# Banks left in one copy on ScalarE, scaled rows in tiles of their own, and routing, census and gathers at other queue places

## The chip, the cores and the metric

The kernel runs on one core of a Trainium2 chip. The metric is the device time of one execution in microseconds (us); the median of three timed runs of the kernel before is 663.76 us (663.69 to 666.47). One more execution was profiled. TensorE is called PE in the rows, VectorE DVE, ScalarE ACT, GpSimd POOL, SyncE SP.

## The reference

Three layers follow each other: a linear attention with a norm, a mixture of eight experts with one expert for each token, and a max-out layer.

```python
kv = np.einsum('bhsd,bhse->bhde', k, v)          # 4 batches, 8 heads, 576 tokens, 64 wide
out = np.einsum('bhsd,bhde->bhse', q, kv)
x = out / sqrt(mean(out * out, -1) + 1e-06) * g_norm   # 2304 tokens x 512
expert_idx = np.argmax(x @ w_gate, axis=1)       # 512 x 8; gate weight from the softmax
# each expert takes its tokens in order, up to its capacity, and computes
y = relu(x @ w1[e]) @ w2[e]                      # 512 x 1024, 1024 x 512
out = gate_w * y[expert_idx, pos]
h = maximum(maximum(out @ m1, out @ m2), out @ m3)   # 512 x 768 each
result = h @ w_out                               # 768 x 512
```

## The kernel before

Each engine works through a queue in the order in which the kernel writes its instructions; waits between engines are semaphores that the framework derives from the tiles. The order is written out by hand.

**Attention, batches 0 to 3.** `kv_step(b)` forms k-transposed times v. `out_step(b)` transposes q and builds `kvx`, the block-diagonal product matrix with eight more columns per head, in which the gate weights are folded, so that one product gives 64 values and 8 gate logits per head (`LW` = 72). A batch has 576 tokens in five slices `s`: slice 0 has 64 rows, slices 1 to 4 have 128. `out_pair(b, u)` makes slices 1 and 2, or 3 and 4, in three groups of heads (three PSUM banks `po`): ScalarE squares the values (`sq`) and copies them to the row tile (`orow`), VectorE copies the logits to `olg` and sums the squares (`ss`). `out_rest(b)` does the same for slice 0.

**Norm and routing.** `stats_steps(b)` is a chain on VectorE (with one square root on ScalarE) that makes the row scales `rnorm`, scales the logits (`lt`, `lg`) and finds each token's expert as a one-hot row (`oh`). `normalise` scales the rows in place: for batches 0 to 2 five GpSimd instructions, for batch 3 split over ScalarE, GpSimd and VectorE. `route(b)` counts with TensorE (`pp`) and a few VectorE instructions where each token goes (`jr`, `pos_i`) and updates the running counts `ohsum`; `census(b)` takes from a product `pc` which expert comes first and how many of its tokens (`pb`) there are. `send(b)` puts five scatters (indirect DMAs that GpSimd issues, rows to `xs` in DRAM) in a list, and `drip` issues one of them behind an instruction of ScalarE, to spread them out.

**The first expert.** Its tokens don't wait for all scatters: for batches 0 and 1 `own_gather` fetches them from `xs` (indirect DMAs to `oxg`, which wait for all scatters so far) and `own_pe` transposes them; for batches 2 and 3 `own_pe` multiplies the scaled rows by 0/1 matrices (`picks`, made by `own`). The four results `px` go to `x0` by `own_out`. `keep_warm` runs idle products on TensorE. Then expert 0 starts (`ph`, the first product of the first layer), and the others follow; their weights come as `raw` tiles by SyncE's queue (four buffers) and are split in two by ScalarE and VectorE.

## Time and profile before

| | before |
|---|---|
| median of three runs | 663.76 us |
| the profiled execution | 663.60 us |
| its span, first to last instruction | 661.8 us |
| TensorE busy | 627.3 us (95%) |
| VectorE, ScalarE, GpSimd busy | 348.2, 270.0, 200.2 us |
| mean granted clock of TensorE | 0.97 |

The span is what the trace shows; 1.8 us of the execution lie around it. A granted clock of 1.00 is 2.4 GHz and one of 0.50 is 1.2 GHz. Busy shares are means over stages that have different limits, so they say where an engine has no room, not what a change is worth.

### The profile page before, as it was taken

Reading aid. Unit: us, or ns where it says so; the run is one execution under the profiler, and the core shown is the slowest. Engines: PE = TensorE matmul, PEld = TensorE weight load, DVE = VectorE, ACT = ScalarE, POOL = GpSimd, SP = SyncE. Lnnn points to the kernel's source line nnn. Section 1 sums busy time; section 2 is a strip of 40 time slices with the busy share of each in tenths; the row PEclk is TensorE's granted clock in tenths of the full one; section 3 lists DMA queues with packets and bytes.
Section 4 is the critical chain, followed back from the end, with each engine's and each line's share of the span. In section 5 each row is a group of like instructions: output and inputs, shape, how many; then the busy total and the mean of one; then the engine's idle time right before and its main releaser. Section 6 shows DMA issues by size and latency. Waiting matters only on the chain.

```text
span 661.8 us, 11400 instructions
## 1 busy us (share of the span) xinstructions
PE 627.3 (95%) x4141; PEld 600.5 (91%) x4141; DVE 348.2 (53%) x755; ACT 270.0 (41%) x619; POOL 200.2 (30%) x280
## 2 busy tenths in 40 slices
PE   7889699999999999999999999999999999999993
PEld 7778599998999999988999989989999999999992
DVE  1587726689898989889975421221231231231220
ACT  1674615685667575766754221121121121121110
POOL 3247553104576867768610001001001001001001
PEclk9999667999999999999999999999999999999997
DMA  8999334796697977887873000000000000000000
GB/s 221 290 280 279 123 116 150 220 298 208 215 273 260 272 239 253 283 248 267 230 202 96 1 17 32 1 17 33 0 17 33 0 17 33 0 17 33 1 16 34
DMA packets 81662, 88.11 MB, mean 133 GB/s; under 512 B 15357, under 2 KB 71165, under 8 KB 81602
## 3 DMA queue, kind: packets, MB, share of 16 engines
q1 hardware_dynamic: 68448, 66.64, 34.5%
q0 software_dynamic: 6240, 14.41, 6.1%
q10 hardware_dynamic: 6914, 6.30, 2.8%
q8 instruction: 34, 0.56, 0.4%
q14 instruction: 26, 0.21, 0.1%
HBM read 71.56 MB, written 15.76 MB: 132 GB/s over the span
## 4 chain that ended last, share of the span: by engine, by line
PE 81%; DVE 7%; DMA 4%; issue 2%; SPq 2%; ACT 2%; ACTq 0%; POOL 0%; POOLq 0%; DVEq 0%
PE pa L767 11%; PE pa L769 11%; PE pa L768 11%; PE ph L769 5%; PE ph L768 5%; PE ph L767 5%; PE py L768 5%; PE py L769 4%; PE py L767 4%; PE pz L1107 4%; PE pz L1106 4%; PE pz L1108 4%; PE px L662 3%; DVE w L298 2%; PE pxt L777 2%
## 5 line engine op out<-in xcount | busy, mean ns | idle before, releaser
L768 PE MATMUL pa<-ys,w 128*128 128x384 f32 x432 | 144.3, 334 | 0.0
L767 PE MATMUL pa<-ys,w 128*128 128x384 f32 x432 | 144.3, 334 | 0.0
L769 PE MATMUL pa<-ys,w 128*128 128x384 f32 x432 | 144.3, 334 | 0.0
L298 DVE TENSOR_TENSOR w<-raw,w 128x512 fp32r<-128x512 f32 x152 | 115.6, 789 | 23.1 <-ACT w L297 22.8
L1111 POOL DMA_INDIRECT out_dram<-o,ctab x18 | 17.5, 972 | 300.1 <-ACT o L1110 297.0
L1094 DVE TENSOR_TENSOR m<-pa,m 128x384 f32<-128x384 f32 x36 | 20.1, 558 | 138.3 <-PE pa L769 138.3
L297 ACT ACTIVATE w<-raw 128x512 fp32r<-128x512 f32 x152 | 89.4, 623 | 5.4 <-DMA raw<-in_moe_w_dram 5.4
L768 PE MATMUL py<-h,w 128*128 128x324 f32 (+7 forms) x256 | 79.9, 312 | 4.0 <-DVE h L791 4.0
L767 PE MATMUL ph<-xt,w 128*128 128x324 f32 (+7 forms) x256 | 80.7, 315 | 1.2 <-DVE xt L669 1.2
L768 PEld LDWEIGHTS pa<-ys,w 128*128 128x128 f32 x432 | 81.1, 188 | 0.2
L767 PEld LDWEIGHTS pa<-ys,w 128*128 128x128 f32 x432 | 81.1, 188 | 0.2
L769 PEld LDWEIGHTS pa<-ys,w 128*128 128x128 f32 x432 | 81.1, 188 | 0.0
L768 PE MATMUL ph<-xt,w 128*128 128x324 f32 (+7 forms) x256 | 80.4, 314 | 0.7 <-DVE xt L680 0.7
L1096 ACT ACTIVATE g<-m 128x384 fp32r<-128x384 f32 x36 | 18.9, 526 | 151.3 <-DVE m L1095 151.3
L769 PE MATMUL ph<-xt,w 128*128 128x324 f32 (+7 forms) x256 | 80.4, 314 | 0.0
L767 PE MATMUL py<-h,w 128*128 128x324 f32 (+7 forms) x256 | 79.9, 312 | 0.0
L769 PE MATMUL py<-h,w 128*128 128x324 f32 (+7 forms) x256 | 79.4, 310 | 0.0
L768 PEld LDWEIGHTS py<-h,w 128*128 128x128 f32 x256 | 48.3, 189 | 5.9 <-DVE h L791 5.9
L920 POOL TENSOR_TENSOR d<-d 128x256 f32<-128x256 f32 x48 | 32.8, 683 | 63.6 <-DVE d L919 15.5
L767 PEld LDWEIGHTS ph<-xt,w 128*128 128x128 f32 x256 | 49.3, 192 | 1.6 <-DVE xt L669 1.5
L768 PEld LDWEIGHTS ph<-xt,w 128*128 128x128 f32 x256 | 49.4, 193 | 1.1 <-DVE xt L680 1.0
L769 PEld LDWEIGHTS ph<-xt,w 128*128 128x128 f32 x256 | 49.3, 193 | 0.0
(252 smaller groups left out, 1055.1 us busy)
## 6 DMA issues: line engine op xcount, KB each, us to landing
raw<-in_moe_w_dram SPq DMA_DIRECT2D x64, 512.0 KB, 3.9
d<-in_moe_w_dram SPq DMA_DIRECT2D x36, 256.0 KB, 5.5
m2w<-dw ACTq DMA_DIRECT2D x36, 128.0 KB, 6.7
raw<-m2w SPq DMA_DIRECT2D x9, 512.0 KB, 4.7
k<-in_k_dram SPq DMA_DIRECT2D x8, 512.0 KB, 7.3
v<-in_v_dram SPq DMA_DIRECT2D x8, 512.0 KB, 9.4
q<-in_q_dram SPq DMA_DIRECT2D x8, 512.0 KB
d<-in_moe_w_out_dram SPq DMA_DIRECT2D x12, 256.0 KB, 5.5
```

Of the source, the lines that this page charges most:

```text
L297: nc.scalar.activation(out=hi, in_=src, func=AF.Copy)
L298: (eng or nc.vector).tensor_tensor(out=lo, in0=src, in1=hi.bitcast(F32), op=ALU.subtract)
L662: nc.tensor.matmul(px[:, dc], osb[b % 3][:n, s, 2 * dc:2 * dc + 2].rearrange("p h d -> p (h d)"), picks[b][:n, s], start=j == 0 and dc == ...
L767: nc.tensor.matmul(po, lhi, rhi, start=first, stop=False)
L768: nc.tensor.matmul(po, lhi, rlo, start=False, stop=False)
L769: nc.tensor.matmul(po, llo, rhi, start=False, stop=last)
L920: nc.gpsimd.tensor_tensor(out=lo.bitcast(F32), in0=hi.bitcast(F32), in1=lo.bitcast(F32), op=ALU.mult)
L1094: nc.vector.tensor_tensor(out=m_, in0=pa[1][:, :YB], in1=m_, op=ALU.max)
L1096: nc.scalar.activation(out=t_[:, 0], in_=m_, func=AF.Copy)
L1106: nc.tensor.matmul(po, h_[:, 0], w_[:, 0], start=c == 0, stop=False)
L1107: nc.tensor.matmul(po, h_[:, 0], w_[:, 1], start=False, stop=False)
L1108: nc.tensor.matmul(po, h_[:, 1], w_[:, 0], start=False, stop=c == NC2 - 1)
```

## The change

ScalarE's copy of a bank now takes all 72 columns to a new tile `ohl`, and VectorE's copies of the logits are gone; `stats_steps` reads the logits from `ohl`. `normalise` reads `ohl` and writes `orow`, which has two buffers in place of three. Routing, sending and the census product of the batch before are in pair 0 of a batch (hooks), no longer in pair 1 and behind it. Both gathers of the first expert's rows are made in batch 2, with one set of index instructions, ahead of that batch's statistics. In batch 3 the census and `own(2)` are a hook of pair 0, `own_pe` goes in the order 2, 0, 1, and `own_out` of these comes after the routing of batch 3. Three runs of `keep_warm` in batch 3 that were 10, 8 and 8 long are 8, 6 and 4 long. `po_f` and `po_i` are made after the stage.

```diff
@@ -312,13 +312,13 @@
         return wt[NT1 + 18 + c]
 
 
-    orow = [sl_.tile([128, 5, DM], F32, name=f"orow{b_}") for b_ in range(3)]
-    osb = [x.rearrange("p s (h d) -> p s h d", d=D) for x in orow]
+    ohl = [sl_.tile([128, 5, H, LW], F32, name=f"ohl{i}") for i in range(2)]
+    orow = [sl_.tile([128, 5, DM], F32, name=f"orow{i}") for i in range(2)]
     rnorm = [sl_.tile([128, 5, H], F32, name=f"rnorm{b_}") for b_ in range(B)]
-    olg = [sl_.tile([128, 5, H, NE], F32, name=f"olg{i}") for i in range(2)]
     ss = [sl_.tile([128, 5, H], F32, name=f"ss{i}") for i in range(2)]
     for i in range(2):
-        nc.gpsimd.memset(olg[i][D:128, 0], 0.0)
+        nc.gpsimd.memset(ohl[i][D:128, 0], 0.0)
+    for i in range(2):
         nc.vector.memset(ss[i][D:128, 0, :], 1.0)
     ohsum = sl_.tile([128, B + 1, NE], BF16, name="ohsum")
     nc.vector.memset(ohsum[:, 0, :], 0.0)
@@ -342,7 +342,7 @@
             if b == 0 and h % 4 == 0 and s == 1:
                 keep_warm(ps_o.tile([128, 512], F32, tag="po", name=f"warm{h}"), 4 if h else 9)
             if b == B - 1 and h == 4 and s == 1:
-                keep_warm(ps_o.tile([128, 512], F32, tag="po", name="warm3"), 10)
+                keep_warm(ps_o.tile([128, 512], F32, tag="po", name="warm3"), 8)
             l, r_ = (t_[h // 4][:, h % 4, s - 1, :] if s else t_[2][:, h, :] for t_ in (vt, kt))
             o_ = pk[h % 2 * D:h % 2 * D + D, h // 2, :]
             nc.tensor.matmul(o_, l, r_, start=s == 1 and h < 2, stop=s == 0 and h > 5)
@@ -388,7 +388,7 @@
             qT[u] = t_
 
         if b in (0, B - 1):
-            keep_warm(ps_o.tile([128, 512], F32, tag="po", name=f"warmq{b}"), 10 if b == 0 else 8)
+            keep_warm(ps_o.tile([128, 512], F32, tag="po", name=f"warmq{b}"), 10 if b == 0 else 6)
         tr(0)
         tr(2)
         if b == 0:
@@ -409,11 +409,9 @@
         nc.scalar.activation(out=sq, in_=po[:, :, 0:D], func=AF.Square)
         for i in range(2):
             d_ = slice(i * D, i * D + D)
-            i_ = nc.scalar.activation(out=osb[b % 3][0:D, 0, i::2], in_=po[d_, :, 0:D], func=AF.Copy)
+            i_ = nc.scalar.activation(out=ohl[b % 2][0:D, 0, i::2], in_=po[d_], func=AF.Copy)
             nc.vector.tensor_reduce(out=ss[b % 2][0:D, 0, i::2], in_=sq[d_], axis=AX.X, op=ALU.add)
         drip(b, i_)
-        for i in range(2):
-            nc.vector.tensor_copy(olg[b % 2][0:D, 0, i::2], po[i * D:i * D + D, :, D:LW])
 
     class Pair:
 
@@ -443,11 +441,8 @@
             nc.scalar.activation(out=self.sq[:, h0:h1], in_=self.po[g][:, :, :, 0:D], func=AF.Square)
 
         def copy(self, g):
-            return nc.scalar.activation(out=self.at(osb, g).rearrange("p r h c -> p h r c"),
-                                        in_=self.po[g][:, :, :, 0:D], func=AF.Copy)
-
-        def logits(self, g):
-            nc.vector.tensor_copy(self.at(olg, g).rearrange("p r h c -> p h r c"), self.po[g][:, :, :, D:LW])
+            return nc.scalar.activation(out=self.at(ohl, g).rearrange("p r h c -> p h r c"),
+                                        in_=self.po[g], func=AF.Copy)
 
         def reduce(self, g):
             h0, h1 = self.groups[g]
@@ -462,7 +457,6 @@
                 hooks[g]()
             pr.square(g)
             drip(b, pr.copy(g))
-            pr.logits(g)
         nc.vector.tensor_reduce(out=ss[b % 2][:, 1 + 2 * u:3 + 2 * u, :].rearrange("p r h -> p h r"),
                                 in_=pr.sq, axis=AX.X, op=ALU.add)
 
@@ -488,7 +482,7 @@
         V.scalar_tensor_tensor(out=r_, in0=u, scalar=1.5, in1=r0, op0=ALU.add, op1=ALU.mult)
         yield
         lt = tmp("lt", [H, NE])
-        V.tensor_tensor(out=lt, in0=olg[b % 2][:, t0:t1], in1=r_.unsqueeze(3).to_broadcast([128, n, H, NE]),
+        V.tensor_tensor(out=lt, in0=ohl[b % 2][:, t0:t1, :, D:LW], in1=r_.unsqueeze(3).to_broadcast([128, n, H, NE]),
                         op=ALU.mult)
         yield
         l_, m_ = lg[:, b, t0:t1], mx[:, b, t0:t1]
@@ -510,13 +504,16 @@
     def rows_of(s):
         return 128 if s else D
 
-    def normalise(o_, r_, n, eng):
-
+    def normalise(b, s, eng):
+
+        n = rows_of(s)
+        i_ = ohl[b % 2][:n, s, :, 0:D]
+        o_, r_ = orow[b % 2][:n, s].rearrange("p (h d) -> p h d", d=D), rnorm[b][:n, s]
         if eng is nc.scalar:
             for h in range(H):
-                nc.scalar.activation(out=o_[:n, h], in_=o_[:n, h], func=AF.Copy, scale=r_[:n, h:h + 1])
+                nc.scalar.activation(out=o_[:, h], in_=i_[:, h], func=AF.Copy, scale=r_[:, h:h + 1])
         else:
-            eng.tensor_tensor(out=o_[:n], in0=o_[:n], in1=r_[:n].unsqueeze(2).to_broadcast([n, H, D]), op=ALU.mult)
+            eng.tensor_tensor(out=o_, in0=i_, in1=r_.unsqueeze(2).to_broadcast([n, H, D]), op=ALU.mult)
 
     def bc(x, n):
         return x.unsqueeze(1).to_broadcast([128, n, NE])
@@ -540,7 +537,7 @@
         n = rows_of(s)
         i_ = nc.gpsimd.indirect_dma_start(
             out=xs, out_offset=IndirectOffsetOnAxis(ap=pos_i[:n, b, s:s + 1], axis=0),
-            in_=orow[b % 3][:n, s].bitcast(I32), in_offset=None)
+            in_=orow[b % 2][:n, s].bitcast(I32), in_offset=None)
         tc.declare_no_dep(i_.ins, group="xs", reason="every token has a row of its own")
         tc.add_to_no_dep_group("xs", i_.ins)
         xs_scatters.append(i_)
@@ -587,20 +584,21 @@
 
     oxg = {}
 
-    def own_gather(b):
+    def own_gather():
 
         V = nc.vector
-        u_, m_ = (sl_.tile([128, 1], F32, tag=x, bufs=2, name=f"{x}{b}") for x in ("og_u", "og_m"))
-        i_ = sl_.tile([128, 1], I32, tag="og_i", bufs=2, name=f"og_i{b}")
-        V.tensor_scalar(out=u_, in0=slot[:, 0:1], scalar1=pb[:, b:b + 1], scalar2=None, op0=ALU.add)
-        V.tensor_scalar(out=m_, in0=u_, scalar1=pb[:, b + 1:b + 2], scalar2=None, op0=ALU.is_lt)
+        u_, m_ = (sl_.tile([128, 2], F32, name=x) for x in ("og_u", "og_m"))
+        i_ = sl_.tile([128, 2], I32, name="og_i")
+        V.tensor_scalar(out=u_, in0=pb[:, 0:2], scalar1=slot[:, 0:1], scalar2=None, op0=ALU.add)
+        V.tensor_tensor(out=m_, in0=u_, in1=pb[:, 1:3], op=ALU.is_lt)
         V.scalar_tensor_tensor(out=m_, in0=u_, scalar=eb0, in1=m_, op0=ALU.add, op1=ALU.mult)
         V.tensor_scalar_add(i_, m_, float(ZROW))
-        xg = oxg[b] = sa.tile([128, DM], F32, tag="oxg", bufs=2, name=f"oxg{b}")
-        g_ = nc.gpsimd.indirect_dma_start(
-            out=xg[:RB[b]].bitcast(I32), out_offset=None, in_=xs,
-            in_offset=IndirectOffsetOnAxis(ap=i_[:RB[b], 0:1], axis=0))
-        after(g_, xs_scatters, "rows come from every scatter")
+        for b in range(2):
+            oxg[b] = sa.tile([128, DM], F32, tag="oxg", bufs=2, name=f"oxg{b}")
+            g_ = nc.gpsimd.indirect_dma_start(
+                out=oxg[b][:RB[b]].bitcast(I32), out_offset=None, in_=xs,
+                in_offset=IndirectOffsetOnAxis(ap=i_[:RB[b], b:b + 1], axis=0))
+            after(g_, xs_scatters, "rows come from every scatter")
 
     def census_pe(b):
         pc_ = ps_kv.tile([128, NE], F32, tag="pm", name=f"pc{b}")
@@ -659,7 +657,7 @@
         for j, s in enumerate(SORD):
             n = rows_of(s)
             for dc in range(NDC):
-                nc.tensor.matmul(px[:, dc], osb[b % 3][:n, s, 2 * dc:2 * dc + 2].rearrange("p h d -> p (h d)"),
+                nc.tensor.matmul(px[:, dc], orow[b % 2][:n, s, dc * 128:(dc + 1) * 128],
                                  picks[b][:n, s], start=j == 0 and dc == 0, stop=j == 4 and dc == NDC - 1)
         return px
 
@@ -683,42 +681,42 @@
     SORD = (0, 4, 1, 2, 3)
     load_batch(1)
     kv_step(0)
+    pcs = {}
+
+    def routes(b):
+        route(b)
+        send(b)
+
+    def census_of(b):
+        pcs[b] = census_pe(b)
+
     for b in range(B - 1):
         qT = out_step(b)
-        out_pair(b, 0, qT)
-        out_pair(b, 1, qT, (lambda: route(b - 1),) if b else ())
-        if b:
-            send(b - 1)
+        out_pair(b, 0, qT, (lambda: routes(b - 1), lambda: census_of(b - 1)) if b else ())
+        out_pair(b, 1, qT)
         out_rest(b, qT)
         load_batch(b + 2)
         if b:
-            census(b - 1, census_pe(b - 1))
+            census(b - 1, pcs[b - 1])
         if b == 1:
             raw_upto(4)
+        if b == 2:
+            own_gather()
         for _ in stats_steps(b, 0, 5, rnorm[b]):
             pass
         for s in range(5):
-            normalise(osb[b % 3][:, s], rnorm[b][:, s], rows_of(s), nc.gpsimd)
+            normalise(b, s, nc.gpsimd)
         kv_step(b + 1)
     b = B - 1
     qT = out_step(b)
-    pcs = []
-
-    out_pair(b, 0, qT, (lambda: route(b - 1), lambda: pcs.append(census_pe(b - 1))))
-    own_gather(0)
-    own_gather(1)
-    census(b - 1, pcs[0])
-    own(b - 1)
-    send(b - 1)
-    nc.vector.tensor_tensor(out=po_f, in0=pb[:, 0:B], in1=roc, op=ALU.min)
-    nc.vector.tensor_copy(po_i, po_f)
+    out_pair(b, 0, qT, (lambda: routes(b - 1), lambda: census_of(b - 1), lambda: (census(b - 1, pcs[b - 1]), own(b - 1))))
     out_rest(b, qT)
     steps = stats_steps(b, 0, 5, rnorm[b])
     pr = Pair(b, 1, qT)
     for g in range(3):
         pr.product(g)
         pr.square(g)
-    pxs = [own_pe(b_) for b_ in range(B - 1)]
+    pxs = {b_: own_pe(b_) for b_ in (2, 0, 1)}
     for g in range(3):
         pr.reduce(g)
         if g < 2:
@@ -726,17 +724,12 @@
     next(steps)
     next(steps)
     drip(b, pr.copy(2))
-    pr.logits(0)
-    pr.logits(1)
     next(steps)
-    pr.logits(2)
     for _ in steps:
         pass
     for s, eng in zip(SORD, (nc.scalar, nc.scalar, nc.gpsimd, nc.gpsimd)):
-        normalise(osb[b % 3][:, s], rnorm[b][:, s], rows_of(s), eng)
-    for b_ in range(B - 1):
-        own_out(b_, pxs[b_])
-    keep_warm(ps_o.tile([128, 512], F32, tag="po", name="warm6"), 8)
+        normalise(b, s, eng)
+    keep_warm(ps_o.tile([128, 512], F32, tag="po", name="warm6"), 4)
     pc = ps_kv.tile([128, NE], F32, tag="pm", name="pc")
     route(b)
     nc.tensor.matmul(pc, ones, ohsum[:, b, :], start=True, stop=False)
@@ -745,7 +738,9 @@
     keep_warm(ps_o.tile([128, 512], F32, tag="po", name="warm7"), 3)
     own(b)
     send(b)
-    normalise(osb[b % 3][:, SORD[4]], rnorm[b][:, SORD[4]], 128, nc.vector)
+    normalise(b, SORD[4], nc.vector)
+    for b_ in (2, 0, 1):
+        own_out(b_, pxs[b_])
     split_next(4)
     own_out(b, own_pe(b))
     while pending:
@@ -1021,6 +1016,8 @@
             nc.scalar.activation(out=t_[:, 0], in_=src, func=AF.Copy)
             nc.vector.tensor_tensor(out=t_[:, 1], in0=src, in1=t_[:, 0].bitcast(F32), op=ALU.subtract)
 
+    nc.vector.tensor_tensor(out=po_f, in0=pb[:, 0:B], in1=roc, op=ALU.min)
+    nc.vector.tensor_copy(po_i, po_f)
     own_at = [nc.values_load(po_i[0:1, b_:b_ + 1], engines=[act], min_val=0, max_val=RO[b_]) for b_ in range(1, B)]
 
     ct_gen, rk_gen = ct_compute(), ranking()
```

On GpSimd, around the statistics of batch 2: `orow_219` and `orow_220` are the rows of batches 1 and 2 before, L519 scales them, L541 scatters them, L600 gathers.

```order
L541 DMA xs<-orow_219,pos_i 18433x512
L547 MEMSET dummy 1x1
L519 TENSOR_TENSOR orow_220<-orow_220,rnorm_223 64x512
L519 TENSOR_TENSOR orow_220<-orow_220,rnorm_223 128x512 x4
L541 DMA xs<-orow_219,pos_i 18433x512
```
```order
L600 DMA oxg_1120<-xs,og_i_1115 72x512
L600 DMA oxg_1129<-xs,og_i_1124 84x512
L541 DMA xs<-orow_220,pos_i 18433x512
L547 MEMSET dummy 1x1
L541 DMA xs<-orow_220,pos_i 18433x512
```

The first piece has batch 1's first scatter ahead of batch 2's scaling, the other four behind it, and the second piece the gathers behind all of these. In the changed kernel `orow_221` holds the rows of batch 1, and `orow_220` those of batch 2.

```order
L538 DMA xs<-orow_221,pos_i 18433x512
L544 MEMSET dummy 1x1
L598 DMA oxg_915<-xs,og_i 72x512
L598 DMA oxg_917<-xs,og_i 84x512
L516 TENSOR_TENSOR orow_220<-ohl_218,rnorm_224 64x512
L516 TENSOR_TENSOR orow_220<-ohl_218,rnorm_224 128x512 x4
L538 DMA xs<-orow_220,pos_i 18433x512
```

All five scatters of batch 1 (the last is the first row) and both gathers now stand ahead of batch 2's scaling.

On TensorE, at the end of batch 3's products, before:

```order
L438 MATMUL po_1171<-kvx_128,qT_1059 128x144 x2
L657 MATMUL px_1175<-ident,oxg_1120 128x72 x4
L657 MATMUL px_1180<-ident,oxg_1129 128x84 x4
L662 MATMUL px_1185<-pick_1136,orow_220 128x84 x20
L331 MATMUL warm_1265<-ident 128x128 x8
L534 LDWEIGHTS ones
```

and in the changed kernel, the waits included:

```order
L436 MATMUL po_1134<-kvx_128,qT_1043 128x144
L660 MATMUL px_1138<-pick_1099,orow_220 128x84 [waits PE_49,DVE_49,Activation_49,Pool_49]
L660 MATMUL px_1138<-pick_1099,orow_220 128x84 x3
L660 MATMUL px_1138<-pick_1099,orow_220 128x84 [waits Pool_49]
L660 MATMUL px_1138<-pick_1099,orow_220 128x84 x15
L655 MATMUL px_1159<-ident,oxg_915 128x72 [waits DMASW2_49,PE_49,Activation_49]
L331 MATMUL warm_1215<-ident 128x128 [waits PE_49,Activation_49]
```

Batch 2's product, which waits for GpSimd (its first four matmuls for slice 0, the rest for slice 4), now stands ahead of the transposes, which wait for the gathers.

## Rows read from the trace of the kernel before

**Rows 1.** Two stages by windows: each engine's busy us, TensorE's clock, DMA share, GB/s

```profile
60.00:101.00 41.00, 33.44 (x234) 31.36 (x232) 21.73 (x66) 17.25 (x49) 23.69 (x37) 0.70 0.44 150
101.00:135.00 34.00, 33.27 (x206) 32.91 (x207) 23.71 (x63) 20.68 (x49) 9.14 (x8) 0.91 0.61 186
```

**Rows 2.** The chain that ended last, in order of time: start us, us, what

```profile
76.91 0.79 PE px L657 x4
77.70 8.98 PE px L662 x40
86.69 3.39 PE warm L331 x16
90.07 0.28 PE pp L534 x11
...
91.91 7.89 PE px L662 x40
...
101.02 0.64 PE ph L767
...
116.74 9.13 DMA raw<-in_moe_w_dram
```

**Rows 3.** TensorE's timeline: start us, us, group, in brackets the idle time before it

```profile
50.60 1.49 PE L438 MATMUL po<-kvx,qT 128*128 128x144 f32 x10 [2.54 <-DVE qT L384]
...
75.48 0.71 PE L657 MATMUL px<-ident,oxg 72*128 72x72 f32 x4 [4.94 <-DVE ms L478]
```

**Rows 4.** Short windows (columns as in rows 1) with TensorE's clock, third column from the right

```profile
47.90:50.60 2.70, 0.16 (x2) 0.00 (x0) 2.60 (x6) 1.16 (x4) 2.53 (x3) 1.00 1.16 210
70.50:75.40 4.90, 0.04 (x1) 0.00 (x0) 4.60 (x20) 1.31 (x4) 1.99 (x2) 0.73 0.18 59
...
77.70:86.60 8.90, 8.90 (x42) 8.75 (x42) 2.47 (x8) 4.03 (x16) 7.19 (x12) 0.50 0.35 122
...
92.00:93.20 1.20, 1.20 (x10) 1.11 (x11) 1.20 (x3) 0.00 (x0) 0.60 (x1) 1.00 0.00 0
93.40:99.80 6.40, 6.38 (x30) 6.16 (x29) 1.44 (x3) 0.00 (x0) 4.73 (x10) 0.50 0.80 251
101.00:106.80 5.80, 5.78 (x21) 5.78 (x22) 1.50 (x7) 1.48 (x3) 0.95 (x1) 0.50 0.07 28
107.00:110.00 3.00, 3.00 (x22) 3.00 (x21) 2.90 (x13) 2.16 (x5) 0.00 (x0) 1.00 0.02 5
```

**Rows 5.** GpSimd's timeline: start us, us, group

```profile
59.23 5.34 POOL L519 TENSOR_TENSOR orow<-orow,rnorm 64x512 f32<-64x512 f32 x5 [1.42 <-DVE rnorm L488]
...
68.61 0.97 POOL L541 DMA_INDIRECT xs<-orow,pos_i  x1 [0.22 <-ACT orow L446]
...
72.32 1.03 POOL L600 DMA_INDIRECT oxg<-xs,og_i  x1 [2.65 <-DVE jl L581]
73.66 0.96 POOL L600 DMA_INDIRECT oxg<-xs,og_i  x1 [0.30 <-issue]
```

**Rows 6.** DMA issues in 53 to 66 us, then in 64 to 92 us: count, us to landing

```profile
xs<-orow,pos_i POOLq DMA_INDIRECT x4, 6.4
...
xs<-orow,pos_i POOLq DMA_INDIRECT x9, 2.7
```

**Rows 7.** VectorE's timeline: one instruction of two batches, `pick`, the end of batch 3's chain

```profile
44.56 1.42 DVE L491 TENSOR_TENSOR lt<-olg,rnorm 128x320 f32<-128x320 f32 x1
...
71.91 0.60 DVE L585 TENSOR_TENSOR pick<-col,jl 128x420 f32<-128x420 f32 x1
...
76.93 0.49 DVE L491 TENSOR_TENSOR lt<-olg,rnorm 128x320 f32<-128x320 f32 x1
...
79.14 0.20 DVE L507 TENSOR_TENSOR oh<-revb,rm 128x40 bf16<-128x40 f32 x1
```

**Rows 8.** Lines 446 and 450: duration ns min/median/max, first and last start, forms

```profile
L446 ACT ACTIVATE orow<-po x24: 364/485/592, 21.2 to 75.7; 128x384 f32<-128x384 f32 x16, 128x256 f32<-128x256 f32 x8
...
L450 DVE COPY olg<-po x12: 190/192/208, 35.1 to 54.7; 128x48 f32<-128x48 f32 x8, 128x32 f32<-128x32 f32 x4
```

## Prediction

> **What bounds the kernel now.** The page gives TensorE 95% of the span, so I looked for the stretches in which its time is not work at full speed. The windows by stage show one: from 60 to 101 us, the end of the attention, TensorE is busy 33.4 of 41 us at a mean clock of 0.70 [rows 1]. The chain of waits, read in order of time, runs through just this stretch on TensorE: transposes `px` at 76.91, the product `px` of batch 2 for 8.98 us, idle products for 3.39, the routing product `pp`, the product `px` of batch 3 for 7.89, and then, at 101.02, the first product `ph` of expert 0 [rows 2]. All that follows waits for that product, so the question is when it starts.
>
> TensorE's timeline shows what opens the stretch: 4.94 us idle until 75.48 [rows 3]. The row names VectorE, but the instruction it ends at is the transpose of gathered rows; the gathers were issued at 72.32 and 73.66 [rows 5], so it is their landing that is waited for. The short windows then show the second loss. During that idle time the clock falls (mean 0.73), and it is 0.50 all through batch 2's product [rows 4]. At 92.0 us it is 1.00 again, and at 93.4 it is 0.50 once more. An idle time of 2.54 us earlier [rows 3] left it at 1.00 [rows 4]. A row of the product costs 8.98 / 40 = 0.22 us at 1.2 GHz [rows 2], and 1.20 / 10 = 0.12 at 2.4 GHz [rows 4].
>
> **The change part by part.** *The copies.* VectorE loses its logit copies, 0.19 us each [rows 8]; with three in each pair and two for slice 0 that is 1.5 us of a batch. ScalarE's copies grow by an eighth of their columns: a 384-wide copy of 0.485 us and a 256-wide one of 0.364 [rows 8] give 0.12 / 128, about 1 ns a column, so 48 columns cost 0.045 us and a batch 0.3. I count neither on the path. In batches 1 and 2 the pairs are paced by ScalarE, and the routing product of the batch before, now in pair 0, makes TensorE wait there for the one-hot chain of that batch, which today holds it only from 48.06 to 50.60 [rows 3]. I bound this part by -1.5 us (all that VectorE gives) and +2.5 us (that wait once more), and take 0, with the four shorter idle products in batch 3 paying for ScalarE. The end of batch 3's pairs stays at 70.5 us (75.48 less 4.94) [rows 3].
>
> *GpSimd's queue.* All five scatters of batch 1 and both gathers now stand ahead of batch 2's scaling. The routing of batch 1 can follow the place where TensorE resumes today, 50.60 [rows 3]; I allow 1.8 us for its small instructions, so the first scatter starts at 52.4. At the spacing of two DMA issues, 73.66 - 72.32 = 1.34 us [rows 5], the last starts at 57.7. It lands 6.4 us later while loads stream [rows 6], at 64.1; the gather starts 1.0 after that (72.32 against 68.61 + 2.7) [rows 5, 6], and both take 73.66 + 0.96 - 72.32 = 2.3 us, to 67.4. The scaling of batch 2 queues behind them and takes 5.34 us [rows 5]: it ends at 72.7, where today it ends at 64.6. So the wait for the gathers leaves TensorE and goes to GpSimd, and what is late next is the scaled rows.
>
> The landing time is the term to doubt: 2.7 us without other traffic, 6.4 with it [rows 6]. With 2.7 the scaling would end at 69.0 and nobody would wait. I take 6.4, since the scatters of batch 1 now lie in the same stretch of loads as those which showed it. The Trainium skill, page "DMA: Bandwidth & Descriptors", section "SWDGE vs HWDGE vs iDMA", says that each DMA engine takes turns between the queues that software and hardware descriptors feed. By that rule a scatter pays for the loads beside it, and the two rows agree; 72.7 would stand and 69.0 would not.
>
> *TensorE from 70.5 us.* The first four of the 20 matmuls of batch 2's product need slice 0 alone, scaled by 67.4 + 1.1 = 68.5; they are 8 rows of 0.12 us, to 71.5. Then it idles 1.2 us, to 72.7. That is less than the 2.54 us that left the clock alone, so I let the clock stay: 32 rows, 3.9 us, to 76.6. The transposes are 0.71 + 0.79 us at half clock [rows 2, 3], 0.8 at full: 77.4. Half the idle products are 0.85 us at full clock (3.39 / 4) [rows 2]: 78.2. The routing product needs the one-hot rows of batch 3, ready at 79.3 today [rows 7], and earlier without eight index instructions and the logit copies in that chain: I take 77.5, hidden. From `pp` to the next product pass 91.91 - 90.07 = 1.84 us [rows 2], plus 0.5, as `pick` may now run beside GpSimd's scaling: 80.6. Batch 3's product: I keep its 7.89 us, with the clock falling after the small products of the routing as it does now: 88.5. From its end to `ph` pass 101.02 - 99.80 = 1.22 us [rows 2]: 89.7.
>
> *Contention.* The same VectorE instruction `lt` takes 1.42 us beside GpSimd's scaling and 0.49 without it [rows 7]. The scaling of batch 2 moves from batch 2's statistics, where it costs VectorE some 2 us, to beside batch 2's `pick`, 0.60 today and 0.60 x 1.42 / 0.49 = 1.7 then [rows 7]. It delays the one-hot rows of batch 3 by 1.1 us, which the 77.5 holds. The Trainium skill, "GPSIMD Engine Reference", section "Key points", states that GpSimd shares its SBUF interfaces with VectorE and collides with instructions that have two SBUF inputs. It speaks against this move. `pick` has two such inputs, so by that rule the 1.1 us is paid; by a reading in which only `lt` suffers it is not, and the sum is the same, for the routing product waits for TensorE either way.
>
> *The sum.* 101.0 - 89.7 = 11.3 us. Expert 0 and all behind it are taken to move along: the weights' buffers are freed by splits which move too. The profiled execution took 663.6 us (span 661.8 and 1.8 around it), next to the median of 663.76; 663.6 - 11.3 = 652.3, and I say **652.5 us**.
>
> **The rivals.** *The clock falls all the same* while the product waits for the scaled rows. Then 32 rows cost 7.2 us (to 79.9), the transposes 1.5, the idle products 1.7, the routing 1.84, batch 3's product 7.89, the end 1.22: `ph` at 94.0, 7.0 us gained, **656.6**. For it speaks that today's fall came in the same place; against it that today's gap is four times as long.
>
> *The clock stays up to the end.* Batch 3's product takes 40 x 0.12 = 4.8 us instead of 7.89, and `ph` starts at full clock, where 22 rows take 3.0 us rather than 21 in 5.8 [rows 4]; its first 12 save 1.7, before VectorE paces the stage. Together 4.8 more: **647.5**. Against it: the clock now falls right behind the routing [rows 4], and that piece is unchanged.
>
> *The gain is hidden further on.* Between 101 and 135 us the chain has 9.13 us of waiting for a weight load [rows 2]. If the loads did not move along with `ph`, half could be lost: **658**. Against it: DMA is busy 0.44 of 60 to 101 us and 0.61 of the next stage [rows 1], so there is room to load earlier.
>
> *Slower: the gathers hold GpSimd's queue too long.* With a half clock, `ph` comes 21.4 us after the scaling ends (7.2 + 1.5 + 1.7 + 1.84 + 7.89 + 1.22), so the change loses once that end lies beyond 79.6, that is, when batch 1's scatters land 13 us after their issue instead of 6.4. At 18 us it would be **668**. The scatters go into a stretch in which loads already fill the DMA engines (share 1.16 at 47.9 to 50.6) [rows 4], which speaks for it; no row shows such a landing time. The same case holds that pair 0's new wait for the routing repeats in each batch.
>
> **How the numbers follow.** The forecast has 0.42, the falling clock 0.24, the steady clock 0.13, the hidden gain 0.13 (half of it within 0.5% of before), slower 0.08 (most of it by over 0.5%). 0.5%, 3.3 us, is about what a measurement of this kernel can tell from no change. So faster 0.84, same 0.10, slower 0.06. From the forecast the range goes down to the steady clock, 647.5, and up past the falling clock and into the hidden gain, **647.5 to 659**; left out are the slower case, part of the hidden gain and the tail of the steady clock.
>
> **What would show it.** Right: on GpSimd the gathers wait some 6 us, and batch 2's scaling ends near 72 to 73; TensorE idles under 2 us between the pairs and batch 2's product, whose rows cost 0.12 us; `ph` starts near 90. Wrong: a window at 0.50 over batch 2's product; that product waiting beyond 75 us; the pairs of batch 3 ending later than 71; or `ph` early but the second expert's products at today's time.

## The result and the profile after

The changed kernel takes 655.84 us (median of 4 runs, 653.05 to 658.73); the kernel before, run beside it, 664.38 (663.69 to 666.47). The ratio is 0.9867, 95% interval 0.9818 to 0.9915. In a later comparison it was 0.9853 (0.9804 to 0.9903). The forecast was 652.5, its range 647.5 to 659. The profiled execution took 655.94 us, 7.7 less than the one of before.

The windows of the two stages of [rows 1], columns as there:

```profile
60.00:101.00 41.00, 36.82 (x271) 34.83 (x270) 28.95 (x69) 23.70 (x61) 24.20 (x31) 0.83 0.46 152
101.00:135.00 34.00, 31.80 (x204) 30.73 (x203) 25.02 (x59) 21.42 (x52) 8.00 (x7) 1.00 0.89 261
```

The end of the attention now runs at a mean clock of 0.83 in place of 0.70, and holds work of expert 0. The next stage has the full clock, yet TensorE is busy 31.8 of 34 us where it was 33.3, and the DMA share is 0.89 where it was 0.61.

TensorE's timeline in the changed stage, which answers to [rows 2, 3]:

```profile
71.81 8.85 PE L660 MATMUL px<-pick,orow 64*128 64x84 f32 x40 [3.34 <-DVE pick L582]
80.45 1.25 PE L655 MATMUL px<-ident,oxg 72*128 72x72 f32 x8
81.49 1.99 PE L331 MATMUL warm<-ident 128*128 128x128 f32 x8
...
85.36 4.96 PE L660 MATMUL px<-pick,orow 64*128 64x84 f32 x40
90.95 0.42 PE L762 MATMUL ph<-xt,w 128*128 128x324 f32 x1 [0.63 <-ACT xt L666]
```

The 4.94 us ahead of the transposes are gone; in their place batch 2's product waits 3.34 us for `pick`, and it runs at half clock (0.22 us a row) as it did before. Batch 3's product takes 4.96 us, the full clock, where it took 7.89 [rows 2]. The first product of expert 0 starts at 90.95 and not at 101.02: 10.07 us earlier.

VectorE's timeline, which answers to [rows 7]:

```profile
45.34 0.90 DVE L494 TENSOR_TENSOR eq<-lg,mx 128x40 f32<-128x40 f32 x1
46.28 0.97 DVE L496 TENSOR_TENSOR eq<-eq,revw 128x40 f32<-128x40 f32 x1
...
65.39 5.64 DVE L578 TENSOR_SCALAR jl<-jr,base,pb 128x5 f32<-128x5 f32 x1
71.06 0.60 DVE L582 TENSOR_TENSOR pick<-col,jl 128x420 f32<-128x420 f32 x1
...
78.22 1.57 DVE L494 TENSOR_TENSOR eq<-lg,mx 128x40 f32<-128x40 f32 x1
```

and GpSimd's, which answers to [rows 5]:

```profile
43.84 5.35 POOL L516 TENSOR_TENSOR orow<-ohl,rnorm 64x512 f32<-64x512 f32 x5 [1.80 <-DVE rnorm L482]
...
63.69 0.98 POOL L598 DMA_INDIRECT oxg<-xs,og_i  x1 [6.83 <-DMA xs<-orow,pos_i]
64.97 0.96 POOL L598 DMA_INDIRECT oxg<-xs,og_i  x1 [0.30 <-DVE pos_i L572]
65.95 5.04 POOL L516 TENSOR_TENSOR orow<-ohl,rnorm 64x512 f32<-64x512 f32 x5
```

The two rows to read together are `jl` at 65.39 and the scaling at 65.95. `jl` subtracts 128x5 numbers, 0.28 us where nothing is beside it; here it takes 5.64 and ends at 71.03, when the last of GpSimd's five scalings ends (70.99). `pick`, the sums of squares and all of VectorE's queue stand behind it. In batch 1 the same five scalings (43.84 to 49.19) let `eq` through after 0.90 and 0.97 us, one scaling each.

Behind the stage some of the gain is lost. Expert 1's inputs (`xt` on ScalarE):

```profile
122.89 1.95 ACT L677 ACTIVATE xt<-pxt,g 128x374 fp32r<-128x374 f32 x4
155.66 1.88 ACT L677 ACTIVATE xt<-pxt,g 128x354 fp32r<-128x354 f32 x4
```

and the same two before:

```profile
132.97 1.95 ACT L679 ACTIVATE xt<-pxt,g 128x374 fp32r<-128x374 f32 x4
163.31 1.88 ACT L679 ACTIVATE xt<-pxt,g 128x354 fp32r<-128x354 f32 x4
```

The first row of each is expert 1, now 10.08 us earlier; the second is expert 2, 7.65 earlier. Between them a weight load holds ScalarE for 2.14 us at 131.17. From 143 to 146 us VectorE is busy for 2.90 us and TensorE for only 1.43, as VectorE's copies of `h` come late, and the clock falls for some 3 us at 147. In what order these cause each other is not shown.

### The profile page after: what moved, and what is told of

Its sections match the earlier page's. It is cut to its first block, busy times and chain, and to the rows that moved or that the text cites. A ratio compares the mean times of both kernels' runs of the same rounds, so it can differ in the third digit from the quotient of the medians.

```text
span 654.2 us, 11325 instructions
## 1 busy us (share of the span) xinstructions
PE 624.2 (95%) x4125; PEld 596.1 (91%) x4125; DVE 346.0 (53%) x719; ACT 270.8 (41%) x619; POOL 202.5 (31%) x280
## 4 chain that ended last, share of the span: by engine, by line
PE 76%; DVE 9%; DMA 7%; issue 2%; ACT 2%; SPq 2%; ACTq 0%; POOL 0%; DVEq 0%; POOLq 0%
PE pa L762 11%; PE pa L764 11%; PE pa L763 11%; PE py L763 5%; PE py L764 5%; PE py L762 4%; PE pz L1104 4%; PE pz L1103 4%; PE pz L1105 4%; DMA raw<-in_moe_w_dram 3%; DVE w L298 3%; PE ph L764 3%; PE ph L763 3%; PE ph L762 3%; PE px L660 2%
## 5 line engine op out<-in xcount | busy, mean ns | idle before, releaser
L298 DVE TENSOR_TENSOR w<-raw,w 128x512 fp32r<-128x512 f32 x152 | 114.1, 779 | 26.8 <-ACT w L297 26.2
L763 PE MATMUL ph<-xt,w 128*128 128x324 f32 (+7 forms) x256 | 79.6, 311 | 0.8 <-DVE xt L678 0.6
L762 PE MATMUL ph<-xt,w 128*128 128x324 f32 (+7 forms) x256 | 79.4, 310 | 0.6 <-ACT xt L666 0.6
L764 PE MATMUL ph<-xt,w 128*128 128x324 f32 (+7 forms) x256 | 79.4, 310 | 0.0
L763 PEld LDWEIGHTS py<-h,w 128*128 128x128 f32 x256 | 48.8, 191 | 9.3 <-DVE h L786 9.1
L763 PEld LDWEIGHTS ph<-xt,w 128*128 128x128 f32 x256 | 48.3, 189 | 1.4 <-DVE xt L678 0.9
L762 PEld LDWEIGHTS ph<-xt,w 128*128 128x128 f32 x256 | 48.3, 189 | 0.9 <-ACT xt L666 0.8
L762 PEld LDWEIGHTS py<-h,w 128*128 128x128 f32 x256 | 48.7, 190 | 0.2
```

Of the source, the lines that this page charges most:

```text
L298: (eng or nc.vector).tensor_tensor(out=lo, in0=src, in1=hi.bitcast(F32), op=ALU.subtract)
L762: nc.tensor.matmul(po, lhi, rhi, start=first, stop=False)
L763: nc.tensor.matmul(po, lhi, rlo, start=False, stop=False)
L764: nc.tensor.matmul(po, llo, rhi, start=False, stop=last)
```

## The experiments

All ratios are to the kernel before, run on the same chip in the same comparison, with 95% intervals. One warning for reading the traces: in the profiled executions of the runs from `e5_both` on, except `e6_step_behind_sums`, batch 3 is reached 6 to 11 us later than in the first profiles (its routing of batch 2 at 69.7 to 74.5 instead of 63.6), since the clock falls, or TensorE stands still, already in batches 1 to 3. So times from the start compare only within one profile.

### The row step in another form: `e1_step_as_tensor_tensor`

```diff
-        nc.vector.tensor_scalar(out=jl, in0=jrs[b], scalar1=base0, scalar2=pb[:, b:b + 1],
-                                op0=ALU.subtract, op1=ALU.subtract)
+        nc.vector.tensor_tensor(out=jl, in0=jrs[b], in1=nb[:, b:b + 1].to_broadcast([128, 5]), op=ALU.subtract)
```

> The changed kernel, with the step jl of own (a tensor-scalar instruction with two pointer scalars, 5.64 us in the changed kernel's trace) written as one tensor-tensor subtraction; the sum of the two scalars is made earlier by a small instruction of its own. Theory (GpSimd's scaling of batch 2 holds that form of instruction until all five of its instructions are done): jl takes at most 1.3 us and pick at most 1.7, pick ends by 68.6 us instead of 71.6, the one-hot rows of batch 3 end near 78 instead of 80.5, batch 2's product still waits for the scaled rows until about 71. The gain over the changed kernel is 1 to 6 us, by whether TensorE's clock then falls. Rival (jl waits for its data, and the profile counts that as busy): jl still ends near 71, and the time is that of the changed kernel, 655 to 657.

Measured: 652.64 us, 0.9845 (0.9802 to 0.9888). VectorE's row in this kernel:

```profile
65.01 5.27 DVE L579 TENSOR_TENSOR jl<-jr,nb 128x5 f32<-128x5 f32 x1
```

GpSimd's five scalings run from 65.21 to 70.25, and the step ends at 70.28. So it is not the form of the instruction, and the theory fell. That the step waits for its data is not it either: in the changed kernel, here and in `e6_step_behind_sums` it ends with the scalings, wherever these lie. The median is 3.2 us under the changed kernel's, within the gain that the theory gave but not for its reason, since batch 2's product still takes 9.02 us at half clock; the two ratios' intervals overlap, so the gain itself is not shown. In this execution the clock does not fall in expert 1, and expert 2's inputs come at 150.76 instead of 155.66.

### The gathers behind the scaling: `e2_gathers_behind_scaling`

```diff
-        if b == 2:
-            own_gather()
     b = B - 1
     qT = out_step(b)
+    own_gather()
```

> The changed kernel, with both gathers made at the start of batch 3 instead of in batch 2, so that they stand behind the scaling of batch 2 in GpSimd's queue. Theory (the gathers' wait for the scatters is what makes the scaling late, and the late scaling holds VectorE and TensorE): the scaling runs from about 58 to 64, jl takes 0.3 us, batch 2's product starts within 0.5 us of the end of batch 3's pairs (near 68.5) at 0.12 us a row, expert 0 starts near 84 instead of 91, and the time is 648 to 652. Rival 1 (weight loads set the pace of experts 0 and 1): expert 0 starts near 84 all the same, but the rows of expert 2 are ready at 154 to 156 as in the changed kernel, and the time is 654 to 656. Rival 2 (the gathers land too late for the transposes): TensorE idles over 3 us ahead of the transposes.

Measured: 654.73 us, 0.9879 (0.9829 to 0.9929), single runs from 643.36 to 658.82. The profiled one is the fastest, 8.2 us under the next. TensorE there:

```profile
68.28 4.85 PE L660 MATMUL px<-pick,orow 64*128 64x84 f32 x40
72.97 0.71 PE L655 MATMUL px<-ident,oxg 72*128 72x72 f32 x8
...
76.45 4.82 PE L660 MATMUL px<-pick,orow 64*128 64x84 f32 x40 [0.66 <-DVE pick L582]
81.90 0.42 PE L761 MATMUL ph<-xt,w 128*128 128x324 f32 x1 [0.63 <-ACT xt L666]
```

With the scaling at 57.33 to 62.60, `jl` takes 0.28 us at 65.27, nothing is waited for ahead of batch 2's product, it runs at full clock, and `ph` comes at 81.90, 9 us earlier than in the changed kernel. The cause of the wait is shown: with the scaling out of the way it is gone, and so is the half clock of batch 2's product. Yet the median is no better. The other five runs have a lower mean clock (0.970 to 0.980 against 0.991); none of them was profiled, so why is not shown. The median lies in the range of rival 1, but the profiled run does not show what that rival says: expert 2's inputs come at 143.20 there. Rival 2 fell: TensorE does not idle ahead of the transposes.

### The least of the bases early: `e3_po_early`

```diff
     out_rest(b, qT)
+    nc.vector.tensor_tensor(out=po_f, in0=pb[:, 0:B], in1=roc, op=ALU.min)
+    nc.vector.tensor_copy(po_i, po_f)
```

> The changed kernel, with po_f and po_i made behind out_rest of batch 3, as early as before, instead of at the start of expert 0. Theory (ScalarE's three register loads wait for po_i, and its first activation of expert 0 queues behind them): the first h comes 1 us earlier after the start of expert 0 (3.3 us after it at most 2.4). The time falls by 0.5 to 1. Rival (weight loads set the pace behind it): h comes earlier, and the time is unchanged within 0.5 us.

Measured: 654.92 us, 0.9872 (0.9824 to 0.9920). The first `h` comes 2.55 us behind the first product (92.88 and 90.33) and not 3.33 (94.28 and 90.95). The ratio is that of the changed kernel; the 0.5 to 1 us of the theory would be too small for these intervals, so theory and rival are not told apart.

### One part alone: `e4_copies_alone` and `e8_places_alone`

`e4_copies_alone` is the kernel before with only the part on copies and tiles (`ohl`, two `orow`, the `normalise` of the change); `e8_places_alone` is before with only the new places:

```diff
-    out_pair(b, 0, qT, (lambda: route(b - 1), lambda: pcs.append(census_pe(b - 1))))
...
+    out_pair(b, 0, qT, (lambda: routes(b - 1), lambda: census_of(b - 1), lambda: (census(b - 1, pcs[b - 1]), own(b - 1))))
...
-    pxs = [own_pe(b_) for b_ in range(B - 1)]
+    pxs = {b_: own_pe(b_) for b_ in (2, 0, 1)}
```

> The kernel before, with only the copies changed: banks copied whole by ScalarE, no logit copies, scaled rows in two tiles of their own; all queue places and idle products as before. Theory (the queue places bring the gain): expert 0 starts at 99.5 to 101, TensorE still idles 4 to 5.5 us ahead of the transposes, and the time is 662 to 664.5. Rival (the copies bring it, by VectorE's shorter chain): expert 0 starts by 97, and the time is below 660.

> The kernel before with the new queue places alone: values and logits keep their two copies and the rows are scaled in place in three buffers. Theory (the parts add up): the whole ratio 0.987 over the copies' 0.994 leaves 0.993, median near 659; scaling of batch 2 still behind the gathers, row step of batch 2 held to its end. Rival 1 (the places bring nothing without the copies, since VectorE's logits copies stand between): 663, as before. Rival 2 (the places are the whole gain): 656.

Measured: the copies 659.06 us, 0.9941 (0.9906 to 0.9975); the places 656.25, 0.9869 (0.9799 to 0.9939). The places alone measure as much as the whole change, as their rival 2 has it. Added up, the parts would give 0.981, and with intervals this wide that is not ruled out. With the copies alone TensorE still waits for the gathered rows, and batch 3's product runs at full clock; with the places alone, in a profile that reached it late, that product runs at the half clock of before. TensorE in the copies alone, two rows, and in the places alone:

```profile
75.15 0.71 PE L653 MATMUL px<-ident,oxg 72*128 72x72 f32 x4 [4.21 <-DMA oxg<-xs,og_i]
...
91.64 4.82 PE L658 MATMUL px<-pick,orow 64*128 64x84 f32 x40 [0.52 <-DVE pos_i L571]
```

```profile
91.00 7.81 PE L663 MATMUL px<-pick,orow 64*128 64x84 f32 x40 [0.66 <-DVE pos_i L575]
```

So for the copies the theory was right about the wait and wrong about the time: `ph` comes at 97.09, 3.93 us ahead of before, and the median is in the rival's range. Of the 3.93 us, 3.05 are batch 3's product. Batch 3's pairs end at 70.94 (75.15 - 4.21), against 70.54 before and 68.47 in the changed kernel: their earlier end does not come from the copies.

### Both edits: `e5_both`

This is `e2_gathers_behind_scaling` with the edit of `e3_po_early`.

> The gathers of batches 0 and 1 behind the scaling of batch 2, and the least of the bases back ahead of the last batch's statistics. Theory (the scaling no longer waits for the scatters, so it is over by 62.6 as in the run with the gathers alone moved; the row step of batch 2 takes 0.3 us, batch 2's rows start at 68.3 without idle time, first product of expert 0 near 82, and the first copy of h 2.6 us behind it in place of 4.6): about 4.6 - 2.6 = 2 us under the run with the gathers alone, median near 652.5. Rival (behind the first product, the clock's falls and the weight loads set the pace): same as that run, median near 654.7 with single runs from 643 to 659.

Measured: 655.35 us, 0.9850 (0.9792 to 0.9908). The forecast of the rival came, no more than with one edit; the 2 us of the theory are less than the interval can tell. In its profile too batch 2's product starts without a wait (77.35) and takes 4.85 us, and the scalings (66.35 to 71.63) let VectorE through.

### When the step is issued: `e6_step_behind_sums`

```diff
-    out_pair(b, 0, qT, (lambda: routes(b - 1), lambda: census_of(b - 1), lambda: (census(b - 1, pcs[b - 1]), own(b - 1))))
+    out_pair(b, 0, qT, (lambda: routes(b - 1), lambda: census_of(b - 1), lambda: census(b - 1, pcs[b - 1])))
     out_rest(b, qT)
+    own(b - 1)
```

> As changed, but the row step and the pick of batch 2 stand on VectorE behind the sums of squares, so that the row step is issued in the midst of GpSimd's five scalings and not just ahead of them. Theory A (a VectorE instruction issued while a scaling runs gets in when that one ends, as the eq of batch 1 at 45.34 with 0.90 us): row step at 68.3 for at most 1.1 us, pick to 70, batch 2's rows at 70 with 1.5 us of idle time, the clock may stay up (4.9 us) or fall (8.9). Rival B (it is held to the end of all five, whenever issued): row step ends at 71.0 again, rows of batch 2 at 71.8, 8.9 us. Either way the squares of pair 1 no longer wait for the sums (72.88 before), so the one-hot of batch 3 is done near 76 in place of 80.3. Median 652 by A, 655 by B.

Measured: 657.27 us, 0.9871 (0.9794 to 0.9949). VectorE:

```profile
67.24 1.22 DVE L460 TENSOR_REDUCE ss<-sq 128x16 f32<-128x1024 f32 x1 [0.67 <-ACT sq L441]
68.38 0.83 DVE L413 TENSOR_REDUCE ss<-sq3r 64x4 f32<-64x256 f32 x2
69.22 2.52 DVE L578 TENSOR_SCALAR jl<-jr,base,pb 128x5 f32<-128x5 f32 x1
```

GpSimd's scalings run from 66.67 to 71.70. The step, issued in their midst, is held past the next end to 71.74, the end of all: rival B. The reductions, of one input, pass beside them unhindered. Batch 2's product starts at 72.52 and takes 9.02 us, as B says; the one-hot rows of batch 3 end at 77.82, earlier than in the changed kernel (80.49) and later than expected.

### Filling the wait: `e7_fill_the_wait`

```diff
+    keep_warm(ps_kv.tile([128, 512], F32, tag="pm", name="warm5"), 12)
     pxs = {b_: own_pe(b_) for b_ in (2, 0, 1)}
```

> As changed, with 12 idle products (24 matmuls, 3.3 us at the full clock by the 0.14 us of one) into a bank of the key-value pool ahead of batch 2's rows, where TensorE was idle for 3.34 us. Theory (that the wait let the clock fall is what it costs; the wait itself is hidden by work that is due anyway): batch 2's rows still start at 71.8, take 4.9 us in place of 8.85, transposes at 76.5, and since the one-hot of batch 3 is there at 80.5 the first product comes near 88.5 instead of 90.95: median 2 to 3 us under the changed kernel's, 653. Rival (the clock falls there whatever TensorE does): rows 8.9 us, first product 91, median 656.

Measured: 656.67 us, 0.9865 (0.9796 to 0.9935), no gain. But its profile does not show the case: batch 3 came late, and another instruction met the scalings (70.38 to 75.41), ahead of the pairs:

```profile
70.73 4.72 DVE L549 TENSOR_TENSOR ohsum<-ohsum,oht 128x8 bf16<-128x8 bf16 x1
```

So this run does not settle whether idle products would have saved the clock there. `e8_places_alone` shows the same (`ohsum` 5.02 us beside the scalings from 71.74).

### Gaps between the scalings: `e9_breaks` and `e12_probe_between`

```diff
             normalise(b, s, nc.gpsimd)
+            if b == 2:
+                nc.gpsimd.memset(dummy, 0.0)
```

and, in the second, three probes ahead of batch 2's routing:

```diff
+    def probe(b):
+        for i in range(3):
+            t_ = sl_.tile([D, 8], F32, name=f"probe{i}")
+            nc.vector.tensor_tensor(out=t_, in0=orow[b % 2][:D, 0, i * 8:i * 8 + 8], in1=rnorm[b][:D, 0], op=ALU.mult)
...
+    out_pair(b, 0, qT, (lambda: (probe(b - 1), routes(b - 1)), lambda: census_of(b - 1), lambda: (census(b - 1, pcs[b - 1]), own(b - 1))))
```

> As changed, with a memset of one number (0.09 us) behind each of GpSimd's five scalings of batch 2. In the runs so far the first VectorE instruction with two inputs in SBUF that comes near these scalings, when they stand behind the gathers, waits for all five (5.64 and 5.27 us for two forms of the row step, 4.72 and 5.02 for another one, 2.52 when it is issued in the midst), while behind a wait for VectorE the scalings let one through each. Theory (five scalings that follow each other without a gap leave no room; a gap lets VectorE in): row step held 1.2 us at most, batch 2's rows at 68.5 without idle time, 4.9 us, first product near 86, median about 652. Rival (it is the issue ahead of the run that binds, a gap of 0.1 to 0.3 us changes nothing): held for 5 to 6.5 us, rows of batch 2 at 72 to 73, first product near 92, median 656.

> The run with breaks (a memset of one number behind each of the five scalings of batch 2), in which the one VectorE instruction that met the scalings met only the last, with three probes more: products of 64x8 from SBUF on VectorE that read the first scaled row tile of batch 2 and stand ahead of batch 2's routing, so that the first of them is issued when the first scaling is over and four are to come (its time is no version to keep: the probes delay the routing). Theory (a gap between GpSimd's instructions lets VectorE in): each probe is held 1.1 us at most, so that the three end within 3.3 us, before the last scaling does. Rival (behind the gathers VectorE waits for the end of the run, gaps or not): the first probe is held for about 4.1 us, to the end of the fifth scaling within 0.1 us, and the two behind it take 0.2 us each.

Measured: the gaps alone 657.06 us, 0.9882 (0.9838 to 0.9927); in the profile only the fifth scaling was met, which tells nothing. The probes (659.61, 0.9961, 0.9923 to 0.9998) settle it. Lines of orow and probe in 60 to 76 us: duration ns min/median/max, first and last start:

```profile
L516 POOL TENSOR_TENSOR orow<-ohl,rnorm x5: 1033/1035/1056, 69.6 to 73.7; 128x512 f32<-128x512 f32 x4, 64x512 f32<-64x512 f32 x1
L696 DVE TENSOR_TENSOR probe<-orow,rnorm x3: 150/152/3704, 71.1 to 74.8; 64x8 f32<-64x8 f32 x3
```

The first probe is held for 3.70 us, from 71.09 to 74.79; the fifth scaling ends at 74.77. The other two take 0.15. A gap of a memset does not let VectorE in: the rival held, and my theory fell.

### Idle products against the falls, and the change again: `e10_fills`, `e11_after_again`

`e10_fills` is `e5_both` with

```diff
-        if b in (0, B - 1):
+        if b != 2:
-            keep_warm(ps_o.tile([128, 512], F32, tag="po", name=f"warmq{b}"), 10 if b == 0 else 6)
+            keep_warm(ps_o.tile([128, 512], F32, tag="po", name=f"warmq{b}"), (10, 4, 0, 6)[b])
...
-    keep_warm(ps_o.tile([128, 512], F32, tag="po", name="warm7"), 3)
+    keep_warm(ps_o.tile([128, 512], F32, tag="po", name="warm7"), 6)
...
     own_out(b, own_pe(b))
+    keep_warm(ps_o.tile([128, 512], F32, tag="po", name="warm8"), 3)
```

> The run with both (gathers behind the scaling, the least of the bases early) with idle products more: 4 ahead of batch 1's queries, 6 in place of 3 ahead of batch 3's rows, 3 behind them. Over all runs so far the time follows the mean granted clock (0.01 of it about 5 us), and at one clock this form stands 4 us under the changed kernel. Theory (the falls of the clock come behind TensorE's short waits and filling these keeps it up): mean clock 0.985 or more in most runs, median near 648. Rival (the falls come anyway, or the products delay what follows them as much): clock 0.975, median 654.

> The changed kernel as it is, beside the two others on one chip: 656 by its first four runs; its profile shows whether the clock's fall at 71 to 85, behind the held row step, comes again (theory: yes, in every execution, as the step is held in each) and whether the one in expert 1 does (it need not).

Measured: with the fills 654.99 us, 0.9838 (0.9795 to 0.9881); the changed kernel beside it 655.94, 0.9853. The fills do raise the mean clock (0.983 to 0.989), as the theory has it, and the time stays, as the rival has it. In the second profile of the changed kernel the hold is absent. Its chain and then VectorE:

```profile
39.55 4.44 another core or an unknown queue
...
59.20 0.22 PE pk L348
59.42 0.51 issue
59.93 0.31 PE pk L348 x2
60.24 0.42 issue
```

```profile
76.22 0.28 DVE L578 TENSOR_SCALAR jl<-jr,base,pb 128x5 f32<-128x5 f32 x1
```

TensorE was held up in batches 1 to 3 in ways that the profile does not explain, `jl` was due only at 76.22, and the scalings (70.11 to 75.15) were over. So my expectation that the hold comes in every execution was wrong: it comes only where the step is due while the scalings run. That execution lost its time earlier instead and is as long (656.23 us).

**All runs together.** In all 14 profiles the stretch from expert 2's inputs (the second `xt` row above) to the end takes 498.4 to 498.8 us: what they differ by lies ahead of it. The runs of a kernel differ by up to 15 us, and they follow their mean granted clock. A least-squares fit over the 127 runs of these comparisons (one value for each kernel, one slope) gives 5.0 us for 0.01 of clock and leaves 1.5 us unexplained. At a clock of 0.98 it puts, with 95% intervals, before at 660.3 ± 0.6, the copies alone at 658.3 ± 0.9, the places alone at 655.9 ± 1.5, the change at 656.5 ± 0.9, the step as a subtraction (`e1_step_as_tensor_tensor`) at 654.5 ± 1.2, the gathers behind the scaling at 652.1 ± 1.2, both edits at 652.6 ± 1.2 and the fills at 657.6 ± 1.2. By this reckoning `e2_gathers_behind_scaling` stands about 4 us under the changed kernel and gives some 2 back through a lower clock (0.9775 in the mean against 0.981). That is an estimate and not shown: the fit takes the clock as given, and an edit can move the clock. The fills show it. Their clock is 0.0095 above that of `e5_both`, 4.8 us by the slope, and the two take the same time. By measured time no version beats the changed kernel by more than the intervals.

## Why the prediction was right, and what was off

By its own steps, predicted and measured in the profile after:

| step | predicted | measured |
|---|---|---|
| landing of batch 1's scatters, us | 6.4 | 6.9 |
| scaling of batch 2 ends | 72.7 | 70.99 |
| pairs of batch 3 end | 70.5 | 68.47 |
| idle ahead of batch 2's product | 1.2 | 3.34 |
| batch 2's product ends | 76.6 | 80.66 |
| batch 3's product starts | 80.6 | 85.36 |
| its length | 7.89 | 4.96 |
| `ph` | 89.7 | 90.95 |
| gain at `ph` | 11.3 | 10.07 |
| gain at the end | 11.3 | 7.7 |

The measured 655.84 us is 3.3 above the forecast, within its range, and 0.8 from the rival of the falling clock (656.6), so nearer to that rival; `ph` at 90.95 is nearer to the forecast (89.7) than to that rival (94.0). **Right:** the wait for the gathers leaves TensorE for GpSimd (6.83 us there), the landing, the end of the scaling within 2 us, and `ph` within 1.3. That `ph` came out so near is partly luck: two errors of opposite sign lie ahead of it, and of the prediction's own signs "a window at 0.50 over batch 2's product" stood under wrong and came.

**The step that failed** is *Contention*, with the term taken from it in *TensorE from 70.5 us*. I priced the collision at `pick`, 0.6 to 1.7 us, as if it cost one scaling. `pick` itself took 0.60. What collided was the step ahead of it, and it was held for the whole run of five scalings, 5.64 us. The size came from `lt`, which stood in a place where one scaling is waited for. The first eight rows of batch 2's product, which I let start at once, need `pick` too, and no step of the prediction says when it is ready; so the idle time was 3.34 us and the clock fell: this is the rival of the falling clock, by another road. Batch 2's product took 8.85 us where I had it end 3.9 us behind the scaling. In the 14 profiles it runs at half clock (8.85 to 9.05 us) in the six in which TensorE idles ahead of it, or of the transposes ahead of it (2.95 to 4.94 us), and at full clock (4.85 to 5.05) in the eight in which it does not. The Trainium skill, "GPSIMD Engine Reference", section "Key points", as the prediction cites it, named the right two parties; the 5.64 us show that one colliding instruction can cost far more than one scaling.

**A second error hid the first.** I kept batch 3's product at half clock; it ran at full clock and saved 2.9 us, as in the rival of the steady clock. The profiles point to the copies: it took 4.82 us with the copies alone and 7.81 with the places alone, and of the twelve profiles with the copies ten have 4.8 to 5.0 us. The two others, `e5_both` (8.14) and `e7_fill_the_wait` (6.82), show that it is no certain effect; how the copies would bring it is not shown.

**"All behind it move along"** was mis-sized: 7.65 of 10.08 us reach expert 2. The next stage's load share rose from 0.61 to 0.89, a load held ScalarE for 2.14 us, and the clock fell in expert 1. Part of the rival of the hidden gain came true. In `e1_step_as_tensor_tensor` the load share was as high (0.88), there was no such fall, and expert 2 stood 12.55 us ahead of before (163.31 - 150.76), so the loss goes with the clock in that execution, not with the loads alone.

**The copies** at nothing was mis-sized: `e4_copies_alone` took 659.06 us, 0.9941 of before, a gain of 1.7 to 6.2 us by its interval, outside the bound of 1.5; the fit gives them 2.0 ± 1.0 at equal clock. By its profile most of it is the full clock of batch 3's product, so it is in the main the second error over again. (The 0.485 and 0.364 us that I read for the two widths are the median and the least of 24 mixed copies; the means by width are 0.511 and 0.414, which changes nothing in the sum.)

## What to carry to other kernels

Before work is moved on GpSimd, look at what VectorE issues beside its new place, down to the smallest instruction, and where the run follows an indirect DMA on GpSimd's queue, price a collision by the whole run of GpSimd's instructions, not by one. A gain of 10 us at one point is worth what the clock and the loads behind it let through, here three quarters. Where single runs spread by more than the gain, do not read one profile as the kernel; a comparison at equal granted clock helps, but the edit may have moved the clock.

## What the hardware did that I had not expected

*VectorE held for a run.* Where GpSimd goes from an indirect gather or scatter straight into its scalings, the first VectorE instruction that collided waited for the end of the whole run of scalings: 5.64, 5.27, 4.72 and 5.02 us of five, 2.52 from the midst, 3.70 with memsets between them, and 1.57 of the two scalings of batch 3 (`eq` at 78.22, the two ending at 79.73). Where GpSimd had stood idle until VectorE's `rnorm`, the same five let one through after each (0.90, 0.97). The Trainium skill, "SBUF — State Buffer", section "Who interferes with whom", says of VectorE instructions in a 2-port mode that whichever engine issues first keeps the shared ports for its whole instruction and the other is blocked until then; it counts `tensor_tensor` with both inputs in SBUF among those that collide with GpSimd's reads, and says that `tensor_reduce` never does on trn2. The reductions agree (`ss` 1.22 us beside the scalings); the hold over several instructions goes beyond it. What makes the two cases differ stays open: the form of the instruction, its moment of issue and a gap between the scalings are each ruled out above. The traces give one more mark of it. In each of the 37 runs of scalings that let VectorE through, one scaling takes 1.27 to 1.35 us, the one that ran into `lt`; in the 14 that held VectorE none takes more than 1.07. So GpSimd too had waited once where VectorE got in, and not once where it was held. Whether that decides it, or the place in the queue, no run tells apart.

*The spread.* The same program ran with a mean clock from 0.960 to 0.982 (before, 48 runs), 5.0 us for each 0.01, and with stops of TensorE that the trace puts down to issue alone. Which executions get them was not found.
